# Linear attention and gated layers on one core: the last token pair's queries computed as seven block products, and output sums in place of query projections as filling ahead of the output weights

## The chip, the cores and the metric

The kernel runs on one core of a Trainium2 chip. The metric is device microseconds of one execution; lower is better. I name the engines as the profile does: PE is TensorE's matmuls, PEld its weight loads, DVE is VectorE, ACT is ScalarE, POOL is GpSimd, SP is SyncE, which issues the transfers. "L1237" is a line of the kernel that was profiled, so the same code has another number in another kernel.

## The reference, cut to what matters

Two layers are applied twice: a linear-attention layer A, then a gated layer B, on 2048 tokens of width 1024, 32 heads of 32.

```
def _A_ref(x, wqkv, wo):
    qkv = split_heads(x @ wqkv); q, k, v = qkv
    pq, pk = phi(q), phi(k)          # phi(t) = (t+1 if t>0 else exp(t)) + 1e-6
    kv  = einsum("bhsd,bhse->bhde", pk, v)
    z   = einsum("bhsd->bhd", pk)
    num = einsum("bhqd,bhde->bhqe", pq, kv)
    den = einsum("bhqd,bhd->bhq", pq, z)[..., None] + 1e-6
    return merge_heads(num / den) @ wo
x = x + A(layernorm(x)); x = x + B(layernorm(x))      # and both again
```

## The kernel before

In an attention layer, the queries and keys of a pair of token tiles (128 tokens each) are computed as a "quad": a 2 by 2 block product with seven instead of eight block products of 4 matmuls each, so 28 matmuls instead of 32. All pairs of the second layer and the last four of the first go this way, except the **queries of the last pair**, which are held back as four direct projections of 8 matmuls.

Then the keys are folded with the tokens ("G sums", 16 chunks), G with the value weights ("kv products"), and kv, masked to the heads by VectorE, with the output weights wo to give the combined output weights wp. Last come the output sums: 16 token tiles with two halves of 8 matmuls each. The end of that stage is where the held projections serve as filling:

```
            ph = proj("q", *held[0])          # 8 matmuls
            kvt(2 * KT - 1)                   # last kv product, then VectorE masks it
            ph()
            proj("q", *held[1])()             # 8 matmuls
            for g in range(4, 8):             # 4 output weights, 1 matmul each
                wprod(g, [0, 4, 1, 3][g - 4], g % 2 == 0)
            proj("q", *held[2])()
            for g in range(4, 8):
                wprod(NG + g, [0, 2, 1, 3][g - 4], g % 2 == 0)
            proj("q", *held[3])()
            # ...
            def y_grp(i, dh, n):              # output sum: 8 matmuls into one PSUM bank
                # dh 0: VectorE adds x and evicts; dh 1: ScalarE has seeded the bank with x and evicts
```

While the output sums run, the next layernorm runs beside them (statistics on VectorE, 1/sqrt on GpSimd, normalising on ScalarE), each normalised tile is transposed by a transfer, and VectorE builds block sums of the transposed tiles for layer B.

Of the kernel before, what the change touches and what calls it, by code (L numbers as in the profile page):

```python
# [180 lines left out]
def build_kernel(nc, A_x, A_wqkv, A_wo, B_w_gate, B_w_up, B_w_down, out):  # L181
    _, S, D = A_x.shape
    F = B_w_gate.shape[1]
    NST, NSB, KT, NG, NFT, NDH = S // 128, S // 512, D // 128, D // 128, F // 128, D // 512
# [8 lines left out]
    NHOLD = 2  # L193
# [52 lines left out]
    O_WP = RA  # L246
# [39 lines left out]
    P = _Prog(V_TW + 8 * 32)  # L286
# [39 lines left out]
    with ExitStack() as es:  # L326
# [19 lines left out]
        x_res = vb(O_X, NST * D).rearrange("p (i d) -> p i d", d=D)  # L346
        xnT = vh(O_XT, KT * S).rearrange("p (k s) -> p k s", s=S)
# [35 lines left out]
        def psb(b):  # L383
            return ps[:, b, :]
# [5 lines left out]
        B_TP = 3  # L390
        B_G = [0, 4]
        B_KVT = [1, 2]
        B_Z = [5, 6]
        B_YY = [5, 6, 7, 3]
        B_GX = [0, 1]
        B_GY = [2, 3]
# [15 lines left out]
        def r_x(i, lo=0, hi=D):  # L412
            return [(O_X + (i * D + lo) * 2, O_X + (i * D + hi) * 2)]
# [7 lines left out]
        def r_xT(s0, s1):  # L421
            return _seg(O_XT, KT, S * 2, s0 * 2, s1 * 2)

        def r_w(base, lo, hi):
            return _seg(base, KT, D * 2, lo * 2, hi * 2)
# [4 lines left out]
        def mset(ap, v, rng):  # L430
# [5 lines left out]
              rd=R(O_A[0], 1024), pwr=[B_KVT[1]])  # L436
# [473 lines left out]
        def layer_A(lnp, nxt, first):  # L910
            kq_i = [0]
            tok = lnp.order
# [19 lines left out]
            def proj(kind, i, h, mid=None):  # L932
                t, v, c0, base = WSRC[kind]
                bank = B_KQ[kq_i[0] % len(B_KQ)]
                kq_i[0] += 1

                def ev():
                    phi_evac(bank, *dst_of(kind, i, h))
                    if kind == "k" and tok.index(i) % 2 and h:
                        z_pair(tok.index(i) // 2)  # L940

                def part(ks):
                    P.add("pe", lambda e: [e.matmul(psb(bank), xnT[:, k, i * 128:(i + 1) * 128], t[:, k, h * 512:(h + 1) * 512],
                                                    start=(k == 0), stop=(k == KT - 1)) for k in ks],
                          rd=r_xT(i * 128, (i + 1) * 128)[ks[0]:ks[-1] + 1] + r_w(base, h * 512, (h + 1) * 512)[ks[0]:ks[-1] + 1], pwr=[bank])
                if mid == "parts":
                    return part, ev
                for ks in ((range(0, 4), range(4, 8)) if mid else (range(KT),)):
                    P.add("pe", (lambda ks: lambda e: [e.matmul(psb(bank), xnT[:, k, i * 128:(i + 1) * 128], t[:, k, h * 512:(h + 1) * 512],  # L949
                                                                start=(k == 0), stop=(k == KT - 1)) for k in ks])(ks),  # L950
                          rd=r_xT(i * 128, (i + 1) * 128) + r_w(base, h * 512, (h + 1) * 512)[ks[0]:ks[-1] + 1], pwr=[bank])
                    if mid:
                        mid()
                        mid = None
                return ev

            class Quad:
                n = 0

                def __init__(self, kind, p):  # L960
                    n = Quad.n
                    Quad.n += 1
                    self.kind, self.p = kind, p
                    self.X, self.Z, self.Y = QX[n % 2], QZ[n % 2], QY[(n + NPL) % 3]
                    self.u2 = (u2sb[n % 2], R(O_U2[n % 2], 2048))
                    self.u3 = (u3sb, R(O_U3, 2048))
                    self.i, self.i2 = tok[2 * p], tok[2 * p + 1]
# [208 lines left out]
            for p in range(npr, 6):  # L1176
                items += [("k", p), ("q", p)]
            if npr < 8:
                items += [("k", 6), ("k", 7), ("q", 6)]
            jobs = {}  # L1180

            def job(n, j, f):
# [43 lines left out]
                g_part(0, j)  # L1226

            QL = [Quad(kind, p) for kind, p in items]
            held = [(tok[i], h) for i in range(NST - NHOLD, NST) for h in range(2)]

            def g_part(n, j):
                h, jj = n // KT, n % KT
# [26 lines left out]
            def kvt(n):  # L1259
                h, j = n // KT, n % KT  # L1260

                def fn(e):
                    return [e.matmul(psb(B_KVT[h])[:, g * 128:(g + 1) * 128], wvs[j][:, (4 * h + g) * 128:(4 * h + g + 1) * 128],  # L1263
                                     GT[n % 4][:, g * 128:(g + 1) * 128],
                                     start=(j == 0 and g == 0), stop=(j == KT - 1), skip_group_check=True) for g in range(4)]
                P.add("pe", fn, rd=R(O_GT + n % 4 * 1024, 1024) + R(O_WVS[j] + h * 1024, 1024), pwr=[B_KVT[h]])
                if j == KT - 1:
                    P.add("dve", lambda e: e.tensor_tensor(
                        out=kvT[:, 4 * h:4 * h + 4, :], in0=psb(B_KVT[h]).rearrange("p (g c) -> p g c", c=128),
                        in1=mask.unsqueeze(1).broadcast_to([128, 4, 128]), op=ALU.mult),  # L1270
                        prd=[B_KVT[h]], rd=R(O_MASK, 256), wr=R(O_KVT + h * 1024, 1024))
# [16 lines left out]
            def wprod(n, bank, on_act):  # L1288
# [7 lines left out]
                else:  # L1296
                    P.add("dve", lambda e: e.tensor_scalar(out=dst, in0=psb(bank), scalar1=rz[:, g:g + 1], scalar2=None, op0=ALU.mult),
                          prd=[bank], rd=R(O_RZ, 32), wr=wr)

            for n in range(2 * KT):  # L1300
                if n:
                    gchunk(n)
                if first and n % 2 == 0:
                    pack()
                if n == 2:
                    z_final()
                if n == 4:
                    z_col()
                if n >= 1:
                    kvt(n - 1)  # L1310
                if n >= KT + 2:
                    m = n - KT - 2
                    for d in range(2):
                        if m < 4:
                            wprod(d * NG + m, B_Z[d], True)
                if n >= 2 and na[0] < NNORM:
                    norm(tok[na[0]])
                    na[0] += 1
            ph = proj("q", *held[0])
            kvt(2 * KT - 1)  # L1320
            ph()
            proj("q", *held[1])()
            for g in range(4, 8):
                wprod(g, [0, 4, 1, 3][g - 4], g % 2 == 0)
            proj("q", *held[2])()
            for g in range(4, 8):
                wprod(NG + g, [0, 2, 1, 3][g - 4], g % 2 == 0)
            proj("q", *held[3])()

            def y_seed(n):  # L1330
                if n < NST:
                    xs, bank = x_res[:, tok[n], 512:1024], B_YY[(2 * n + 1) % 4]
                    P.add("act", lambda e: e.copy(psb(bank), xs), rd=r_x(tok[n], 512, 1024), pwr=[bank])

            def y_grp(i, dh, n):
                bank = B_YY[(2 * n + dh) % 4]

                def fn(e):
                    return [e.matmul(psb(bank), xnT[:, g, i * 128:(i + 1) * 128], wp[:, g, dh * 512:(dh + 1) * 512],  # L1339
                                     start=(dh == 0 and g == 0), stop=(g == NG - 1), skip_group_check=True) for g in range(NG)]  # L1340
                xs = x_res[:, i, dh * 512:(dh + 1) * 512]
                rx = r_x(i, dh * 512, (dh + 1) * 512)
                P.add("pe", fn, rd=r_xT(i * 128, (i + 1) * 128) + r_w(O_WP, dh * 512, (dh + 1) * 512), pwr=[bank])
                if dh == 0:
                    P.add("dve", lambda e: e.tensor_tensor(out=xs, in0=psb(bank), in1=xs, op=ALU.add), prd=[bank], rd=rx, wr=rx)
                    return
                P.add("act", lambda e: e.copy(xs, psb(bank)), prd=[bank], wr=rx)

            nxt.use_dma = True
            nxt.on_act = YACT  # L1350
            ring_begin(first)
            for _ in range(3):
                ring_issue()
            y_seed(0)
            for i in range(NST):
                if na[0] < NST:
                    if i % 3 == 2:
                        norm(tok[na[0]])
                        na[0] += 1
                elif RG["n"] < NR:  # L1360
                    ring_issue()
                if first and i % 3 == 1:
                    pack()
                nxt.step_t(1)
                nxt.b1_one()
                if 2 <= i < 15:
                    nxt.start(i - 2)
                y_grp(tok[i], 0, i)
                y_seed(i + 1)
                if i < 15:  # L1370
                    nxt.b2_one()
                y_grp(tok[i], 1, i)
                if first and i >= 14:
                    prep_s(i - 14)
                if not first and i >= 8:
                    stash(i - 8)
                if nxt.t_next >= 8 and RG["tq"] is None:
                    RG["tq"] = t_ops(0)
                for _ in range(2 if i > 12 else 1):
                    if RG["tq"]:  # L1380
                        RG["tq"].pop(0)()
# [691 lines left out]
```

## Time and profile before

| | before |
|---|---|
| time, median of 3 runs | 1428.89 us (1428.35 to 1429.38) |
| profiled run | 1428.16 us, span 1426.4 us |
| matmul records / weight loads | 8150 / 8209 |
| first quad to first matmul of layer B, first attention layer | 168.03 us |
| the same, second attention layer | 217.37 us |

Every matmul has one weight load, so 59 matmul records of this trace are lost. That is why I measure stages from the start of one matmul to the start of another and do not count matmul records: the second layer's first quad matmul is one of the lost ones, and it is set one slot (0.216 us) before the first recorded. The prediction shows the lines of the page and of TensorE's timeline that matter; the profiled run of before, at 1428.16 us, was, as it will turn out, faster than every other run of this kernel on record (the next is 1428.35).

### The profile page before, as it was taken

The page shows a single profiled execution, that of the slowest core. Times are in us where ns is not written, and L with a number is a line of the kernel's source. Part 1 is how long each engine was busy: PE and PEld are TensorE (multiplying, and loading weights), DVE is VectorE, ACT ScalarE, POOL GpSimd, SP SyncE. Part 2 cuts the span into 40 slices and gives each one's busy share as a digit, 9 for nine tenths or more (in the row PEclk, how much of TensorE's full clock was granted, in tenths as well). Part 3 has the DMA queues.
Part 4 walks back from the last instruction along what each step waited for, and adds up shares of the span by engine and source line. Part 5 has one row for each costly group of instructions (what it writes and reads, how often), then busy time and mean ns, then how long its engine had stood idle before and what let it go on. Part 6 is the DMA issues. An engine that isn't in the chain of part 4 may idle for free.

```text
span 1426.4 us, 21923 instructions
## 1 busy us (share of the span) xinstructions
PE 1417.6 (99%) x8150; PEld 791.0 (55%) x8209; DVE 1200.9 (84%) x2344; ACT 722.0 (51%) x1471; POOL 153.8 (11%) x197
## 2 busy tenths in 40 slices
PE   9999999999999999999999999999999999999999
PEld 4444444555546566664554444456666475666548
DVE  7897978999978799987689978788888877888888
ACT  5882355444420266655377814567776105777400
POOL 3203521000010000002010045310000100000000
PEclk9999999999999999999999999999999999999999
DMA  7868978997786777768884367767775966777553
GB/s 240 218 141 225 216 179 197 310 311 265 252 264 212 234 254 249 252 228 295 239 281 104 92 177 162 172 196 254 258 246 194 329 221 230 259 258 260 191 205 122
DMA packets 270699, 320.74 MB, mean 225 GB/s; under 512 B 164096, under 2 KB 211072, under 8 KB 270592
## 3 DMA queue, kind: packets, MB, share of 16 engines
q1 hardware_dynamic: 270592, 319.34, 73.2%
q8 instruction: 64, 1.05, 0.3%
q14 instruction: 43, 0.35, 0.1%
HBM read 236.45 MB, written 73.40 MB: 217 GB/s over the span
## 4 chain that ended last, share of the span: by engine, by line
PE 92%; DVE 4%; ACT 2%; issue 1%; DMA 1%; POOL 0%; SPq 0%; DVEq 0%
PE ps L1421 29%; PE ps L1504 17%; PE ps L1853 16%; PE ps L1339 8%; PE ps L1237 8%; PE ps L976 8%; PE ps L1760 5%; DVE arena L808 1%; PE ps L949 1%; DVE arena L811 1%; DVE arena L455 1%; ACT arena L668 1%; DMA arena<-in_A_wqkv_dram 1%; PE ps L1263 1%; PE ps L1290 0%
## 5 line engine op out<-in xcount | busy, mean ns | idle before, releaser
L808 DVE TENSOR_TENSOR arena<-arena 128x512 f16<-128x512 f16 (+7 forms) x1027 | 507.3, 522 | 56.9 <-ACT arena L1508 32.7
L1421 PE MATMUL ps<-arena 128*128 128x512 f16 x1888 | 456.8, 379 | 0.1
L811 DVE SCALAR_TENSOR_TENSOR arena<-ps,arena 128x512 f16<-128x512 f32 (+3 forms) x558 | 358.6, 658 | 86.9 <-PE ps L1853 45.0
L1504 PE MATMUL ps<-arena 128*128 128x256 f16 x2184 | 287.5, 273 | 0.1
L1421 PEld LDWEIGHTS ps<-arena 128*128 128x128 f16 (+1 forms) x1888 | 182.9, 98 | 162.4 <-ACT ps L1450 3.8
L1504 PEld LDWEIGHTS ps<-arena 128*128 128x128 f16 (+1 forms) x2184 | 212.3, 98 | 90.4 <-ACT arena L1508 7.2
L1853 PE MATMUL ps<-arena 128*128 128x512 bf16 (+1 forms) x1048 | 230.6, 379 | 0.8
L1853 PEld LDWEIGHTS ps<-arena 128*128 128x128 f16 x1064 | 104.1, 98 | 123.8
L1426 ACT ACTIVATE arena<-ps 128x512 f32<-128x512 f32 x224 | 133.9, 598 | 76.7 <-PE ps L1421 62.5
L1508 ACT ACTIVATE arena<-ps 128x256 f32<-128x256 f32 x351 | 125.1, 384 | 26.4 <-PE ps L1504 21.5
L976 PE MATMUL ps<-arena 128*128 128x512 f16 (+1 forms) x605 | 134.0, 379 | 1.2 <-ACT arena L983 0.6
L1237 PE MATMUL ps<-arena 128*128 128x512 bf16 x498 | 114.7, 379 | 0.7
L1339 PE MATMUL ps<-arena 128*128 128x512 bf16 x502 | 110.3, 379 | 0.5
L1514 ACT COPY ps<-ps 128x256 f32<-128x256 f32 x182 | 66.3, 364 | 75.5 <-DVE arena L811 28.5
L976 PEld LDWEIGHTS ps<-arena 128*128 128x128 f16 x616 | 59.3, 98 | 74.8 <-ACT arena L983 5.9
L1760 PE MATMUL ps<-arena 128*128 128x256 f16 (+1 forms) x882 | 97.0, 273 | 0.0
L1450 ACT COPY ps<-ps 128x512 f32<-128x512 f32 x112 | 65.4, 583 | 61.5 <-PE ps L1421 51.3
L1078 POOL TENSOR_TENSOR arena<-arena 128x1024 f16<-128x1024 f32 x32 | 77.2, 2413 | 155.7 <-DVE arena L1076 140.8
L1760 PEld LDWEIGHTS ps<-arena 128*128 128x128 f16 x882 | 86.2, 98 | 11.0 <-DVE arena L811 0.2
L1517 DVE TENSOR_TENSOR ps<-ps,arena 128x256 f32<-128x256 f32 x182 | 76.7, 428 | 10.7 <-PE ps L1504 9.5
L1339 PEld LDWEIGHTS ps<-arena 128*128 128x128 f16 x512 | 50.1, 98 | 60.4
L1788 ACT COPY arena<-ps 128x256 f32<-128x256 f32 x8 | 3.0, 373 | 155.8 <-PE ps L1760 155.8
(72 smaller groups left out, 981.0 us busy)
## 6 DMA issues: line engine op xcount, KB each, us to landing
arena<-w_scratch SPq DMA_DIRECT2D x84, 896.0 KB, 4.6
arena<-t_scratch SPq DMA_DIRECT2D x32, 896.0 KB, 5.9
arena<-in_B_w_down_dram SPq DMA_DIRECT2D x24, 896.0 KB, 5.0
arena<-sp_scratch SPq DMA_DIRECT2D x26, 768.0 KB, 4.2
w_scratch<-arena SPq DMA_DIRECT2D x28, 512.0 KB, 6.1
arena<-w_scratch SPq DMA_DIRECT2D x28, 384.0 KB, 4.7
x_scratch<-arena SPq DMA_DIRECT2D x40, 256.0 KB, 5.1
arena<-x_scratch SPq DMA_DIRECT2D x40, 256.0 KB, 4.1
```

What stands on the lines that cost most here:

```text
L808: P.add("dve", lambda e: e.tensor_tensor(out=out, in0=a, in1=b, op=op), rd=rd, wr=wr, prd=prd)
L811: P.add("dve", lambda e: e.scalar_tensor_tensor(out=out, in0=a, scalar=sc, in1=b, op0=ALU.mult, op1=op1), rd=rd, wr=wr, prd=prd)
L976: P.add("pe", lambda e: [e.matmul(psb(bank), a[0][:, k, :], b[0][:, k, :], start=(q in (1, 5) and k == 0), stop=(k == 3), skip_group_check ...
L1078: P.add("pool", lambda e: e.tensor_tensor(out=asb[b].rearrange("p (h c) -> p h c", c=32), in0=pbuf.rearrange("p (h c) -> p h c", c=32), in ...
L1237: return [e.matmul(psb(bank), xrt[t][:, jj * 128:(jj + 1) * 128], pk[:, h, t, :], start=(t == tok[0]), stop=(t == tok[NST - 1])) for t in ts]
L1339: return [e.matmul(psb(bank), xnT[:, g, i * 128:(i + 1) * 128], wp[:, g, dh * 512:(dh + 1) * 512], start=(dh == 0 and g == 0), stop=(g == ...
L1421: P.add("pe", lambda e: [e.matmul(psb(bank), w[:, k, :], x[:, k, :], start=(start and k == 0), stop=(k == 3), skip_group_check=True) for k ...
L1426: P.add("act", lambda e: e.activation(t, psb(bank), AF.Copy, scale=SG), prd=[bank], wr=r)
L1504: P.add("pe", lambda e: [e.matmul(psb(bank)[:, 256 * half:256 * half + 256], w[:, k, :], xx[:, k, :], start=(start and k == 0), stop=(k == ...
L1508: P.add("act", lambda e: e.activation(d, src, AF.Copy, scale=sc), prd=[xk], wr=rd_)
L1760: P.add("pe", lambda e: [e.matmul(psb(bank)[:, 256 * half:256 * half + 256], a[:, k, 128 * r:128 * r + 128], b[:, k, :], start=(start and ...
L1853: P.add("pe", lambda e: [e.matmul(psb(bank), hv[:, 7 * hf + k, t * 128:(t + 1) * 128], w[:, k, :], start=(q in "15" and hf == 0 and k == 0 ...
```

## The change

The intent: the last pair's queries become a quad as well (28 matmuls in place of 32), and the wait for the output weights is filled with the first halves (4 of 8 matmuls) of the output sums of tiles 0 and 1. Those can start early, because the first four output weights of each half are ready long before. Two more PSUM banks stay open meanwhile, so banks are dealt anew.

```diff
-        B_Z = [5, 6]
+        B_Z = [5, 3]
...
-                    self.X, self.Z, self.Y = QX[n % 2], QZ[n % 2], QY[(n + NPL) % 3]
+                    self.X, self.Z, self.Y = QX[n % 2], QZ[n % 2], QY[(n + NPL + 2) % 3]
...
-                items += [("k", 6), ("k", 7), ("q", 6)]
+                items += [("k", 6), ("k", 7), ("q", 6), ("q", 7)]
...
             for n in range(2 * KT):
+                if n == 2 * KT - 1:
+                    y_seed(0)
+                    y_seed(1)
...
-            ph = proj("q", *held[0])
-            kvt(2 * KT - 1)
-            ph()
-            proj("q", *held[1])()
-            (output weights, held[2], output weights, held[3] as shown above)
+            def y_part(n, dh, k):
+                y_mm(n, dh, range(4 * k, 4 * k + 4))
...
+            y_part(0, 0, 0)
+            y_part(0, 1, 0)
+            kvt(2 * KT - 1)
+            y_part(1, 0, 0)
+            for g in range(4, 8):
+                wprod(g, [0, 1, 4, 2][g - 4], g % 2 == 0)
+            y_part(1, 1, 0)
+            for g in range(4, 8):
+                wprod(NG + g, [0, 1, 4, 2][g - 4], g % 2 == 0)
```

(In the loop of output sums, tiles 0 and 1 then run their second halves only; that part is cut.)

More of the change, by code (lines that the diff above doesn't have):

```diff
@@ L1228, in layer_A @@
             QL = [Quad(kind, p) for kind, p in items]
-            held = [(tok[i], h) for i in range(NST - NHOLD, NST) for h in range(2)]
             def g_part(n, j):
@@ L1298, in wprod, with y_seed @@
                           prd=[bank], rd=R(O_RZ, 32), wr=wr)
+            def y_seed(n):
+                if n < NST:
+                    xs, bank = x_res[:, tok[n], 512:1024], B_YY[(2 * n + 1) % 4]
+                    P.add("act", lambda e: e.copy(psb(bank), xs), rd=r_x(tok[n], 512, 1024), pwr=[bank])
             for n in range(2 * KT):
+                if n == 2 * KT - 1:
+                    y_seed(0)
+                    y_seed(1)
                 if n:
@@ L1318, in layer_A, with y_mm @@
                     na[0] += 1
-            ph = proj("q", *held[0])
-            kvt(2 * KT - 1)
-            ph()
-            proj("q", *held[1])()
-            for g in range(4, 8):
-                wprod(g, [0, 4, 1, 3][g - 4], g % 2 == 0)
-            proj("q", *held[2])()
-            for g in range(4, 8):
-                wprod(NG + g, [0, 2, 1, 3][g - 4], g % 2 == 0)
-            proj("q", *held[3])()
-            def y_seed(n):
-                if n < NST:
-                    xs, bank = x_res[:, tok[n], 512:1024], B_YY[(2 * n + 1) % 4]
-                    P.add("act", lambda e: e.copy(psb(bank), xs), rd=r_x(tok[n], 512, 1024), pwr=[bank])
+            def y_mm(n, dh, gs):
+                i, bank = tok[n], B_YY[(2 * n + dh) % 4]
+                P.add("pe", lambda e: [e.matmul(psb(bank), xnT[:, g, i * 128:(i + 1) * 128], wp[:, g, dh * 512:(dh + 1) * 512],
+                                                start=(dh == 0 and g == 0), stop=(g == NG - 1), skip_group_check=True) for g in gs],
+                      rd=r_xT(i * 128, (i + 1) * 128)[gs[0]:gs[-1] + 1] + r_w(O_WP, dh * 512, (dh + 1) * 512)[gs[0]:gs[-1] + 1], pwr=[bank])
+            def y_part(n, dh, k):
+                y_mm(n, dh, range(4 * k, 4 * k + 4))
             def y_grp(i, dh, n):
                 bank = B_YY[(2 * n + dh) % 4]
-                def fn(e):
-                    return [e.matmul(psb(bank), xnT[:, g, i * 128:(i + 1) * 128], wp[:, g, dh * 512:(dh + 1) * 512],
-                                     start=(dh == 0 and g == 0), stop=(g == NG - 1), skip_group_check=True) for g in range(NG)]
+                if n < 2:
+                    y_part(n, dh, 1)
+                else:
+                    y_mm(n, dh, range(NG))
                 xs = x_res[:, i, dh * 512:(dh + 1) * 512]
                 rx = r_x(i, dh * 512, (dh + 1) * 512)
-                P.add("pe", fn, rd=r_xT(i * 128, (i + 1) * 128) + r_w(O_WP, dh * 512, (dh + 1) * 512), pwr=[bank])
                 if dh == 0:
@@ L1353, in layer_A @@
                 ring_issue()
-            y_seed(0)
             for i in range(NST):
@@ L1367, in layer_A @@
                     nxt.start(i - 2)
-                y_grp(tok[i], 0, i)
-                y_seed(i + 1)
+                if i != 1:
+                    y_grp(tok[i], 0, i)
+                if i == 0:
+                    y_grp(tok[1], 0, 1)
+                else:
+                    y_seed(i + 1)
                 if i < 15:
```

## The prediction

> **What bounds the kernel now.** I read the page first, for the busy shares and the chain that ended last, then the list of what TensorE waited for, then the two stretches that the change rewrites, in order of time.
>
> ```profile
> span 1426.4 us, 21923 instructions
> PE 1417.6 (99%) x8150; PEld 791.0 (55%) x8209; DVE 1200.9 (84%) x2344; ACT 722.0 (51%) x1471; POOL 153.8 (11%) x197
> PE 92%; DVE 4%; ACT 2%; issue 1%; DMA 1%; POOL 0%; SPq 0%; DVEq 0%
> ...
> PE ps L435 <- POOL arena L431: 1.4, 1, 1.4
> PE ps L943 <- DMA arena<-in_A_wqkv_dram: 0.7, 2, 0.5
> PE ps L976 <- ACT arena L983: 0.6, 3, 0.2
> ```
>
> TensorE (PE) is busy 99% of the span and carries 92% of the chain. Over the whole span its waits come to 2.7 us, of which 2.1 us are at the start of the kernel. So there is almost no idle time left to win: a change is worth the matmuls that it takes off TensorE, less any new wait.
>
> The stretch in question, first linear-attention layer, from the timeline of TensorE (start, length, engine, line, instructions; the lengths include the drain of the last matmul, so I use differences of starts):
>
> ```profile
> 165.77 3.62 PE L1237 MATMUL ps<-arena 128*128 128x512 bf16 x16
> 169.22 0.39 PE L1263 MATMUL ps<-arena 128*128 128x128 bf16 x4
> 169.44 1.89 PE L949 MATMUL ps<-arena 128*128 128x512 bf16 x8
> 171.17 0.39 PE L1263 MATMUL ps<-arena 128*128 128x128 bf16 x4
> 171.39 1.89 PE L949 MATMUL ps<-arena 128*128 128x512 bf16 x8
> 173.12 1.03 PE L1290 MATMUL ps<-arena 128*128 128x512 bf16 x4
> 174.20 1.67 PE L949 MATMUL ps<-arena 128*128 128x512 bf16 x7
> 175.71 1.03 PE L1290 MATMUL ps<-arena 128*128 128x512 bf16 x4
> 176.57 1.89 PE L949 MATMUL ps<-arena 128*128 128x512 bf16 x8
> ```
>
> L1237 is the last G sum, L1263 the kv products, L949 the four query projections of the last token pair that were held back as filling, L1290 the output weights; the output sums L1339 begin at 178.30. Eight L949 matmuls take 171.17 - 169.44 = 1.73 us, so one slot is 0.216 us; four short ones take 0.22 us. The stretch from 169.22 to 178.30 holds 32 + 8 matmuls of 512 columns (one record is missing, the "x7") and 8 of 128: 40 x 0.2157 + 8 x 0.056 = 9.08 us, and it lasts 9.08 us. The second layer shows the same 9.07 us (878.55 to 887.62). So the wait for the output weights **is already filled without a gap**; the change cannot win there, it can only fill it with other work.
>
> **What the Trainium skill says.** "TensorE: Matmul & The Clock Gate", section "Back-to-back issue gap", gives N/2.4 + 2.5 ns, 216 ns for 512 columns; the trace agrees (0.216 us). The 131 ns that the same section gives for a sustained stream does not appear here. The same page, "Step-by-step: what each phase is for", says that weight loads are pulled ahead of running matmuls; here they start 0.21 us ahead (172.91 against 173.12). "Perfetto Trace Analysis", section "Tensor Engine Instruction (MATMUL, LD_WEIGHTS)", says that matmul ends are estimated, hence my use of starts. "PSUM — Partial Sum Buffer", section "The four PSUM rules", says that writes of ScalarE leave the accumulate bits alone: the second half of an output tile is seeded by a ScalarE copy of x and then summed without a clearing first matmul, and two more banks now stay open across the weight products. This matters for correctness, not time; no run so far shows it.
>
> **The change, part by part (per attention layer; there are two).**
>
> 1. Removed: four direct projections, 4 x 8 = 32 matmuls, 32 x 0.2157 = 6.90 us.
> 2. Added: one more quad (seven block products of 4 matmuls, 28 in all), 28 x 0.2157 = 6.04 us. It needs no new operand sums: the key quad of the same pair makes them already and now keeps them one step longer. Net of 1 and 2: **-4 matmuls, -0.86 us**.
> 3. Moved: 16 of the 256 output-sum matmuls, 3.45 us, from behind the output weights to before and between them. No net change on TensorE.
> 4. The new wait. Before, 1.73 us of queries lie between the last kv product and the first output weight. That weight needs the masked kv matrix. The rows of the timeline between:
>
> ```profile
> 171.59 0.69 DVE L1268 TENSOR_TENSOR arena<-ps,arena 128x512 bf16<-128x512 f32 x1 [1.38 <-PE ps L1263]
> ...
> 176.34 0.10 PEld L1290 LDWEIGHTS ps<-arena 128*128 128x128 bf16 x1 [0.31 <-DVE arena L1297]
> ```
>
> VectorE (DVE) ends the mask at 171.59 + 0.69 = 172.28. A weight load released by VectorE starts 0.05 us after it (L1297 ends at 176.29, the load starts at 176.34) and its matmul hardly later (176.36). So the output weight could have run at about 172.34, which is 1.17 us after the kv products began at 171.17. In the new order there are 0.22 us of kv products and only four output-sum matmuls (0.86 us), 1.09 us in all. **New stall: about 0.09 us.** VectorE is free for it in time: it idled 1.38 us before this row, and the 0.22 us kv group before it sits at the same distance from the last G sum as now.
> 5. The second group of weights reuses banks 0, 1, 4, 2 of the first. Let t be the start of the first. Matmuls end at t+0.38, +0.60, +0.81, +1.03; two VectorE evictions take 1.40 us as a pair (row L1297, "1.40 ... x2" in the timeline), so the last bank is free near t + 0.64 + 1.40 = t + 2.04. It is needed at t + 0.86 + 0.86 + 0.65 = t + 2.37. No stall, 0.3 us to spare, and ScalarE with 1.26 us a pair is earlier. Before, both engines evicted queries in this window as well; that load is gone. The second half of tile 0's second output half needs the weights of the second group: ready near t + 2.32 + 0.04 + 1.40 = t + 3.76, needed at t + 4 x 0.86 + 0.86 = t + 4.3. No stall.
> 6. The extra quad's evictions come in the quad stage, where TensorE has this beside it (columns: stretch, its length, then busy us and count of PE, PEld, DVE, ACT, POOL):
>
> ```profile
> 725.00:815.64 90.64, 89.63 (x410) 40.03 (x417) 80.51 (x200) 72.31 (x132) 4.58 (x10) 1.00 0.48 135
> 169.22:178.30 9.08, 9.03 (x48) 4.29 (x48) 6.57 (x13) 4.69 (x8) 2.48 (x2) 1.00 1.11 200
> ```
>
> Fifteen quads: VectorE 80.51/15 = 5.4 us and ScalarE 72.31/15 = 4.8 us per quad, against 6.04 us of TensorE. Both fit. The 412 matmuls from 725.55 to 815.48 should take 88.87 us and take 89.93: three stalls of some 0.35 us behind ScalarE's copy L983, in quads that also carry layernorm work. The new quad is the last and has none, so I put 0.03 us on it.
> 7. Banks: turning the Y banks by two puts the first quad of the second layer on bank 2. In the preceding layer's last evictions this bank is read by the one that starts at 724.87 and ends at 725.55; the quad needs it at 726.0. No stall.
>
> Sum: 2 x (-0.86 + 0.09 + 0.03) = -1.5 us. **1428.9 - 1.5 = 1427.4 us**, 0.1% faster.
>
> **The rivals.**
> A. A new wait takes the place of the old filling. Filling between kv and the weights is halved, from 1.73 to 0.86 us, and VectorE works in order: one late normalisation (3.3 us of VectorE work per tile) ahead of the mask would show at once. For it: DVE is 84% busy. Against it: it idled 1.4 us (first layer) and 2.1 us (second layer) before the mask. If it holds, up to 0.9 us a layer are lost and the time stays at 1428.9.
> B. The evictions become the bound. The projections needed 4 plain evictions; a quad also needs three PSUM copies on ScalarE. If the last quad lasts 6.9 us in place of 6.04, nothing is gained: 1428.9 to 1429.5. Against it: the loads in step 6.
> C. Relief downstream: fewer evictions in the weights' window, so that the output sums start cleaner. TensorE shows no gap there before, so there is nothing to relieve: same as my number. Even if every wait at L976 (about 1 us with the drain) vanished as well, 1426.3 would be the floor.
> D. Transfers. The reload of a block of query weights, needed by the projections alone, is left in. 512 KB a layer were hidden before and stay hidden; no effect on the time.
>
> **Range and chances.** My centre is the count of matmuls, which is firm, less small stalls, which are not. C bounds it below near 1426.4; A or B in full brings it back to 1428.9. The three runs before span 1.0 us, so I add some on top: 1426.4 to 1428.9. A change of 2% is 28.6 us; the work touched is some 20 us a layer, so faster by 2% is all but excluded, and slower by 2% needs a stall that I have overlooked: 0.003 and 0.007.
>
> **What would show it.** Right: the matmuls of line L949 fall by 64 and those of L976 rise by 56; the stretch from last G sum to the rest of the output sums shrinks from 9.08 to about 5.7 us, with one gap of about 0.1 us ahead of the first output weight, released by the mask on VectorE; the quad stage grows by about 6.0 us; the output sums after the weights shrink by 3.45 us. Wrong: a gap of 0.3 us or more before the output weights or between their groups, new waits of L976 on ScalarE in the last quad, or a first G sum that waits for a bank.

## The result

| | before | after |
|---|---|---|
| median | 1429.14 us (1428.35 to 1429.71, 4 runs) | 1426.71 us (1426.61 to 1427.38, 4 runs) |
| ratio | | 0.9984, 95% interval 0.9967 to 1.0002 |
| first attention layer, first quad to layer B | 168.03 us | 167.26 us |
| second attention layer, same | 217.37 us | 216.57 us |

A ratio is the mean time of one kernel's fast runs over that of the other's of the same rounds, so it is not quite the ratio of the medians.

From the page of after, the head and the busy line:

```profile
span 1425.7 us, 21979 instructions
PE 1419.6 (100%) x8201; PEld 790.6 (55%) x8201; DVE 1201.3 (84%) x2348; ACT 726.9 (51%) x1481; POOL 154.2 (11%) x197
```

There are 8 matmuls fewer (8201 weight loads against 8209), yet PE's busy time rose by 2 us. Nothing got slower: this trace lost no matmul record and the earlier one lost 59. Here the span and the stages say more than the busy sum.

TensorE's timeline of after in the stretch that the prediction shows (start, length, engine, line, count; L1262 is kv, L1328 output sums, L1289 output weights), and then the weight load and the mask at the first output weight, with the idle time before them in brackets:

```profile
175.77 0.39 PE L1262 MATMUL ps<-arena 128*128 128x128 bf16 x4
175.99 1.89 PE L1328 MATMUL ps<-arena 128*128 128x512 bf16 x8
177.72 0.39 PE L1262 MATMUL ps<-arena 128*128 128x128 bf16 x4
177.94 1.03 PE L1328 MATMUL ps<-arena 128*128 128x512 bf16 x4
178.89 1.04 PE L1289 MATMUL ps<-arena 128*128 128x512 bf16 x4
179.76 1.03 PE L1328 MATMUL ps<-arena 128*128 128x512 bf16 x4
...
178.14 0.69 DVE L1267 TENSOR_TENSOR arena<-ps,arena 128x512 bf16<-128x512 f32 x1 [0.35 <-PE ps L1262]
178.89 0.55 PEld L1289 LDWEIGHTS ps<-arena 128*128 128x128 bf16 x4 [0.41 <-DVE arena L1267]
```

Four output-sum matmuls begin at 177.94 and should be issued by 177.94 + 4 x 0.2157 = 178.80; the first output weight starts at 178.89. That is the one gap, 0.085 us in the unrounded starts, released by the mask. Between the two groups of weights there is none (178.89 + 4 x 0.2157 = 179.76). The second layer has the same single gap.

**Where the time went.** The two attention layers are 0.77 and 0.80 us shorter, 1.57 us in all. But the profiled pair differs by only 0.8 us (1428.16 against 1427.38) and the medians by 2.4 us. Three things outside these stages move between runs: the stretch before the first quad (65.2 to 66.1 us over all profiles; 0.51 us longer in this profile of after), the last stage (0.27 us shorter in after), and a gap of 0.55 us at the **hand-over** from the first attention layer to layer B. With the two layers they add up to the 0.8 us of the profiled pair. The timelines of TensorE there, first before, then after (L1421 and L1434 are the same line, layer B's first matmuls):

```profile
237.65 6.65 PE L1421 MATMUL ps<-arena 128*128 128x512 f16 x30
```

```profile
237.82 3.40 PE L1434 MATMUL ps<-arena 128*128 128x512 f16 x15
241.61 2.76 PE L1434 MATMUL ps<-arena 128*128 128x512 f16 x12 [0.39 <-DVE arena L811]
```

Before ran through; after waits for VectorE. From start to start the gap is 0.767 us where one slot is 0.216: 0.55 us lost. What VectorE was doing, from its timeline of after, with its first eviction for layer B (L811) as the last row:

```profile
217.95 0.69 DVE L1345 TENSOR_TENSOR arena<-ps,arena 128x512 bf16<-128x512 f32 x1 [1.07 <-PE ps L1328]
221.33 1.23 DVE L808 TENSOR_TENSOR arena<-arena 128x2048 f16<-128x2048 f16 x1 [2.69 <-DMA arena<-arena]
...
240.87 0.68 DVE L811 SCALAR_TENSOR_TENSOR arena<-ps,arena 128x512 f16<-128x512 f32 x1
```

VectorE sat idle for 2.69 us until a transfer landed, the transpose of the eighth normalised tile, and then worked without a gap until 240.87. In before the same two times are 221.03 and 240.58. So the saving of the first attention layer can be swallowed here. That became the question of the experiments.

### The profile page after: what moved, and what is told of

Its sections match the earlier page's. It is cut to its first block, busy times and chain, and to the rows that moved or that the text cites. A ratio compares the mean times of both kernels' runs of the same rounds, so it can differ in the third digit from the quotient of the medians.

```text
span 1425.7 us, 21979 instructions
## 1 busy us (share of the span) xinstructions
PE 1419.6 (100%) x8201; PEld 790.6 (55%) x8201; DVE 1201.3 (84%) x2348; ACT 726.9 (51%) x1481; POOL 154.2 (11%) x197
## 4 chain that ended last, share of the span: by engine, by line
PE 95%; DVE 3%; DMA 1%; issue 1%; ACT 0%; SPq 0%; DVEq 0%
PE ps L1434 28%; PE ps L1517 17%; PE ps L1866 16%; PE ps L976 9%; PE ps L1236 8%; PE ps L1773 7%; PE ps L1328 6%; PE ps L949 3%; DVE arena L808 1%; DMA arena<-in_A_wqkv_dram 1%; PE ps L1262 1%; PE ps L1289 0%; DVE arena L455 0%; DVE arena L996 0%; PE ps L943 0%
## 5 line engine op out<-in xcount | busy, mean ns | idle before, releaser
L808 DVE TENSOR_TENSOR arena<-arena 128x512 f16<-128x512 f16 (+9 forms) x1035 | 510.4, 521 | 58.0 <-ACT arena L1521 32.8
L1434 PE MATMUL ps<-arena 128*128 128x512 f16 x1888 | 457.0, 379 | 0.5 <-DVE arena L811 0.4
L811 DVE SCALAR_TENSOR_TENSOR arena<-ps,arena 128x512 f16<-128x512 f32 (+3 forms) x558 | 358.1, 657 | 87.3 <-PE ps L1866 44.3
L1434 PEld LDWEIGHTS ps<-arena 128*128 128x128 f16 (+1 forms) x1888 | 183.0, 98 | 162.8 <-ACT ps L1463 3.8
L1866 PEld LDWEIGHTS ps<-arena 128*128 128x128 f16 x1064 | 104.1, 98 | 123.8
L976 PE MATMUL ps<-arena 128*128 128x512 f16 (+1 forms) x672 | 146.8, 379 | 0.6 <-ACT arena L983 0.6
L1236 PE MATMUL ps<-arena 128*128 128x512 bf16 x512 | 116.1, 379 | 0.0
L1328 PE MATMUL ps<-arena 128*128 128x512 bf16 x512 | 111.8, 379 | 0.0
L976 PEld LDWEIGHTS ps<-arena 128*128 128x128 f16 x672 | 64.8, 98 | 81.4 <-ACT arena L983 6.1
L1773 PEld LDWEIGHTS ps<-arena 128*128 128x128 f16 x882 | 86.2, 98 | 11.0 <-DVE arena L811 0.2
L1328 PEld LDWEIGHTS ps<-arena 128*128 128x128 f16 x512 | 49.9, 98 | 59.5
```

The lines of the kernel that those rows point to most:

```text
L808: P.add("dve", lambda e: e.tensor_tensor(out=out, in0=a, in1=b, op=op), rd=rd, wr=wr, prd=prd)
L811: P.add("dve", lambda e: e.scalar_tensor_tensor(out=out, in0=a, scalar=sc, in1=b, op0=ALU.mult, op1=op1), rd=rd, wr=wr, prd=prd)
L976: P.add("pe", lambda e: [e.matmul(psb(bank), a[0][:, k, :], b[0][:, k, :], start=(q in (1, 5) and k == 0), stop=(k == 3), skip_group_check ...
L1236: return [e.matmul(psb(bank), xrt[t][:, jj * 128:(jj + 1) * 128], pk[:, h, t, :], start=(t == tok[0]), stop=(t == tok[NST - 1])) for t in ts]
L1328: P.add("pe", lambda e: [e.matmul(psb(bank), xnT[:, g, i * 128:(i + 1) * 128], wp[:, g, dh * 512:(dh + 1) * 512], start=(dh == 0 and g == ...
L1434: P.add("pe", lambda e: [e.matmul(psb(bank), w[:, k, :], x[:, k, :], start=(start and k == 0), stop=(k == 3), skip_group_check=True) for k ...
```

## The experiments

All variants come from one source with switches. With the switches set as in before and as in after, its instruction sequence on each of the five engines is that of before and of after. Every kernel ran 5 rounds. All outputs are right. "Before" is the kernel before in the same call, on the same chip.

| kernel | median, us | mean | before, mean | ratio | 95% interval |
|---|---|---|---|---|---|
| *first call* | | | | | |
| after_again | 1426.94 | 1427.12 | 1429.18 | 0.9985 | 0.9973 to 0.9998 |
| first_only | 1428.14 | 1428.10 | 1429.18 | 0.9992 | 0.9979 to 1.0005 |
| second_only | 1428.15 | 1427.90 | 1429.18 | 0.9991 | 0.9978 to 1.0003 |
| quad_no_fill | 1432.55 | 1432.87 | 1429.18 | 1.0022 | 1.0008 to 1.0035 |
| *second call* | | | | | |
| before_again | 1429.11 | 1429.24 | 1429.03 | 1.0002 | 0.9988 to 1.0015 |
| no_reload | 1428.03 | 1428.19 | 1429.03 | 0.9994 | 0.9982 to 1.0007 |
| late_noreload | 1427.59 | 1427.81 | 1429.03 | 0.9991 | 0.9979 to 1.0004 |
| relu_split | 1430.50 | 1430.37 | 1429.03 | 1.0009 | 0.9997 to 1.0022 |
| *third call* | | | | | |
| after_third | 1427.73 | 1427.70 | 1429.19 | 0.9989 | 0.9977 to 1.0002 |
| no_reload_2 | 1428.00 | 1428.04 | 1429.19 | 0.9992 | 0.9979 to 1.0004 |
| act_adds | 1427.29 | 1427.34 | 1429.19 | 0.9986 | 0.9972 to 0.9999 |
| before_act_adds | 1429.36 | 1429.37 | 1429.19 | 1.0001 | 0.9988 to 1.0014 |

The means are of all five runs; the ratios agree with their quotient to 0.0001, except for quad_no_fill, where the ratio fits the mean without the slowest run, 1432.33. The intervals are about as wide as the effects, so most conclusions below rest on stages of the profiles, which repeat to 0.03 us where nothing disturbs them. There is one profile for each row, so a row cannot tell its kernel from its run.

From each profile I worked out, from starts of matmuls: **A0** and **A1**, the first and second attention layer from the first quad to layer B's first matmul; **landing**, when VectorE starts its first block sum, counted from the first quad; **gap**, what TensorE loses in the first 9 us of layer B.

| kernel | first layer | A0 | landing | gap | A1 |
|---|---|---|---|---|---|
| before | old | 168.03 | 155.51 | 0 | 217.37 |
| before_again | old | 168.03 | 156.49 | 0.98 | 217.37 |
| second_only | old | 168.03 | 156.15 | 0.64 | 216.60 |
| first_only | new | 167.26 | 155.32 | 0.58 | 217.37 |
| after | new | 167.26 | 155.30 | 0.55 | 216.57 |
| after_again | new | 167.26 | 155.14 | 0.41 | 216.59 |
| after_third | new | 167.26 | 156.05 | 1.29 | 216.59 |
| no_reload | new | 167.44 | 156.24 | 1.32 | 216.59 |
| no_reload_2 | new | 167.28 | 156.01 | 1.24 | 216.59 |
| late_noreload | new | 167.16 | 155.84 | 1.20 | 216.51 |
| relu_split | new | 167.16 | 156.38 | 1.73 | 218.90 |

(The profiles of the third call miss the record of the second layer's first quad matmul; A1 is corrected by one slot there, as for before.)

### The changed kernel again, and each layer alone

after_again is the changed kernel. The other two use the old path in one of the two layers:

```diff
 def layer_A(lnp, nxt, first):
+    new = first          # first_only;  new = not first for second_only
     ...
-    items += [("k", 6), ("k", 7), ("q", 6), ("q", 7)]
+    items += [("k", 6), ("k", 7), ("q", 6)] + ([("q", 7)] if new else [])
     # likewise the banks, the filling and the loop of output sums
```

> The changed kernel again, for a firmer number. Theory 1, count: four matmuls fewer and a 0.085 us stall more per attention layer, all of it kept, 1.5 us faster than before. Theory 2, hand-back: the profile of after shows a new gap of 0.55 us (starts 240.84 to 241.61 in place of one slot) at the hand-over from the first attention layer to the gated layer, where TensorE waits for VectorE, so only about 1.0 us is kept. Theory 3: the 2.4 us between the medians of the first runs are real and something is won that I did not see. Whether the gap near 241 us comes again tells if it belongs to the kernel or to that run.

> The change in the first attention layer alone. Theory 1: 0.77 us faster. Theory 2: the gap at the hand-over (near 241 us) is there, 0.2 to 0.4 us faster. Theory 3: some 1.2 us.

> The change in the second attention layer alone. Theories 1 and 2: 0.6 to 0.8 us faster, no gap at the hand-over in the first layer. Theory 3: some 1.2 us.

Measured by means: 2.06, 1.08 and 1.28 us faster than the kernel before. The parts add up to 2.36, which is 2.06 within the noise, so **each layer carries about half**. The stages of the profiles follow theory 1 exactly: A0 is 167.26 wherever the first layer is new and 168.03 where it is old, A1 216.6 and 217.37. But the gap of theory 2 is also there, and it is there in second_only, whose first layer is the old one. So the change does not cause it: my theory 2, in that form, fell. The gain in the means is larger than 0.77 us a layer, as theory 3 has it, but by less than the half width of the intervals (some 1.8 us), and these three runs do not say why.

### The quad without the filling

```diff
-            y_part(0, 0, 0)
-            y_part(0, 1, 0)
             kvt(2 * KT - 1)
-            y_part(1, 0, 0)
             for g in range(4, 8):
                 wprod(g, [0, 1, 4, 2][g - 4], g % 2 == 0)
-            y_part(1, 1, 0)
             for g in range(4, 8):
                 wprod(NG + g, [0, 1, 4, 2][g - 4], g % 2 == 0)
     # the seeding with x and the loop of output sums are as in before again (cut)
```

> The seven block products for the last pair in both layers, but no output sums ahead of the weights: nothing fills the waits. Worked out from durations in the trace, per layer: the last kv product waits 0.62 us for ScalarE's copy of the G sum, the first output weight 0.95 us for the mask, the second group of weights 0.58 us in all for banks; with 0.86 us fewer matmuls this makes 1.3 us a layer slower, 2.6 us in all. The rival, that the filling matters little because VectorE or the transfers set the end of the stage anyway, expects the same time as before or faster.

It is 3.7 us slower than before by the means of all five runs (3.2 without its slowest, the profiled one at 1435.04 us), and over 5 us slower than the changed kernel. The rival is refuted: the filling carries the change. In the second layer my sum holds: A1 grows from 217.37 to 218.69 us, 1.32 us for an expected 1.3. In the first layer of the profiled run A0 grows by 3.77 us. The timeline there shows the rest (L1281 kv, L1308 output weights, L1286 the mask, L1092 a step of the normalisation on VectorE, L1096 its multiplication on GpSimd):

```profile
176.11 1.91 POOL L1096 TENSOR_TENSOR arena<-arena 128x1024 f16<-128x1024 f32 x1 [2.68 <-DMA arena<-arena]
176.22 1.83 DVE L1092 TENSOR_SCALAR arena<-arena 128x32 f32<-128x32 f32 x1
176.71 0.23 PEld L1281 LDWEIGHTS ps<-arena 128*128 128x128 bf16 x4 [0.62 <-ACT arena L1261]
...
178.36 0.63 DVE L1286 TENSOR_TENSOR arena<-ps,arena 128x512 bf16<-128x512 f32 x1
179.04 0.55 PEld L1308 LDWEIGHTS ps<-arena 128*128 128x128 bf16 x4 [2.11 <-DVE arena L1286]
```

The wait for ScalarE's copy is 0.62 us as reckoned. The wait for the mask is 2.1 us, not 0.95, because a small VectorE step, 0.46 us on average in after, took 1.83 us beside GpSimd's multiplication and stood in front of the mask. (At this place it took 1.54 us in after as well; there it was over before the mask's input was ready.) The Trainium skill, "SBUF — State Buffer", section "Who interferes with whom", describes a port pair that VectorE and GpSimd share as a lock, "the other **fully blocks** (not throttle)"; the row agrees, it ends 0.04 us after GpSimd's; no run here tests it by moving one of the two. The waits seem to have had a second price, from the view by stretches (stretch, its length, busy us of PE, PEld, DVE, ACT, POOL, then granted clock, DMA share, GB/s; the number of instructions in brackets):

```profile
176.00:179.70 3.70, 1.30 (x12) 0.61 (x10) 2.93 (x5) 0.81 (x2) 3.09 (x2) 1.00 1.26 216
179.70:183.20 3.50, 3.37 (x10) 1.04 (x9) 2.91 (x4) 3.21 (x6) 0.74 (x1) 0.55 1.15 284
```

The two waits, close together, were followed by 3.5 us at a clock of 0.55, in which matmuls started every 0.427 us in place of 0.216. That the waits caused it is not shown. It is not so in every run: such a drop takes 0.45 x 3.5 / 1433 = 0.001 off the mean clock of the span, and only the profiled run and one other, the two slowest, have 0.999; the other three have 1.000. So rival A of the prediction is real: with no filling at all it comes true. In the changed kernel the mask had 0.35 us of idle VectorE ahead of it in the first layer; that is how close it is.

### The kernel before as a control

No edit; the kernel before from the common source.

> The kernel before, instruction for instruction, as a control. Its first profile ran 1428.16 us, the fastest of all its runs, and shows no gap at the hand-over from the first attention layer to the gated layer (near 241 us), where four profiles of other kernels show 0.41 to 0.64 us. Theory 2 (the change causes that gap): no gap here either, span of the stages as in the first profile. Theory 2b (the gap belongs to that hand-over and to the run, whatever the kernel; the first profile was a lucky one): a gap of 0.4 us or more here, and the stage between the two attention layers near 492.4 us in place of 492.0. Ratio 1.000 within 0.0006.

The ratio is 1.0002, and the gap is there:

```profile
237.65 3.83 PE L1488 MATMUL ps<-arena 128*128 128x512 f16 x17
242.30 1.90 PE L1488 MATMUL ps<-arena 128*128 128x512 f16 x8 [0.82 <-DVE arena L827]
```

TensorE loses 0.98 us there. Theory 2b holds: **the profile on which the prediction rests was a lucky run**, and the "never waits" that I read from it is not true of the kernel in general.

### The reload of the query weights left out, twice

```diff
-            dma(wq[:, 0:4, 512:1024], wqkv_v[:, 0:4, 512:1024], ..., KW["q"][1])
```

> The changed kernel without the reload of the block of query weights (512 KB a layer), which nothing reads any more. If the gap at the hand-over is a matter of transfer traffic, it shrinks from 0.4 to 0.6 us to under 0.2 us and the time falls by 0.4 us against the changed kernel, to a ratio near 0.9982. If the traffic has nothing to do with it: same gap, ratio 0.9985.

> The changed kernel without the reload, again, now beside the changed kernel on the same chip. In its first run the gap grew to 1.12 us and the ratio was 0.9994, but on another chip than the changed kernel's. If the chip made that, it equals the changed kernel here within 0.0003; if leaving the reload out does it (the transfers behind it move and meet others), the tile lands 0.6 us or more later than in the changed kernel again, gap near 1.1 us, ratio near 0.9992.

The first run went against the expectation: the gap did not shrink, it was 1.32 us. (The 1.12 us in the expectation of the repeat is the second of the two gaps that make it up.) The repeat stood beside the changed kernel on one chip, and there the two are alike: landing 156.01 and 156.05, gap 1.24 and 1.29 us, ratios 0.9992 and 0.9989. So the first run's gap belongs to the chip, the call or the run, which these runs cannot tell apart, and leaving the reload out changed nothing beside the changed kernel, as the prediction's rival D says.

The first run shows something else. Its A0 is 0.18 us longer than in after, because the stall before the first output weight is 0.26 us there in place of 0.085; in no_reload_2 it is 0.10. The small VectorE step of the section on quad_no_fill took 1.78 and 1.54 us in these two, and the mask followed it and the reciprocal without any idle time. So the 0.35 us ahead of the mask can be used up in the changed kernel too: the instructions of all engines but SyncE are the same in no_reload and in after.

### A longer filling before the first output weight

On top of no_reload:

```diff
             y_part(0, 0, 0)
-            y_part(0, 1, 0)
             kvt(2 * KT - 1)
+            y_part(0, 1, 0)
             y_part(1, 0, 0)
```

> As no_reload, and one of the two partial output sums that stand ahead of the last kv product goes behind it, so that the filling before the first output weight is 1.73 us again and before the kv product 1.09 us. My arithmetic of the stall: both gaps of 0.085 us before the output weights vanish, each attention layer is 0.085 us shorter (167.26 and 216.58 us become 167.17 and 216.50). The kv product needs ScalarE's copy of the G sum about 0.85 us after the last G matmul was issued, so 1.09 us is enough. The rival, that the gap comes from something else than the length of the filling, keeps it.

Both gaps are gone (L1281 kv, L1356 output sums, L1308 output weights):

```profile
176.84 0.39 PE L1281 MATMUL ps<-arena 128*128 128x128 bf16 x4
177.07 1.89 PE L1356 MATMUL ps<-arena 128*128 128x512 bf16 x8
178.79 1.03 PE L1308 MATMUL ps<-arena 128*128 128x512 bf16 x4
```

177.07 + 8 x 0.2157 = 178.79 within rounding, with nothing lost. A0 and A1 are 0.10 and 0.06 us shorter than in after, where 0.085 was reckoned; the kv product between the halves did not wait either. The time cannot show 0.2 us.

### Relief for ScalarE in the second layer's quads

On top of late_noreload:

```diff
-    RLB = [(4, 5, 6, 7), (4, 5, 6, 7)]     # banks whose positive part ScalarE takes
+    RLB = [(4, 5, 6, 7), (4, 7)]
```

> As late_noreload, and in the second layer the positive part of one of the two banks of each quad is taken by VectorE straight from PSUM and not by ScalarE's extra pass. If the three gaps of some 0.35 us in the second layer's quads come from ScalarE's queue (4.8 of 6.04 us a quad, plus the layernorm's), they vanish and the second attention layer shrinks by 1.0 us, ratio near 0.9975. The rival: VectorE (5.4 us a quad, some 5.8 then) becomes what TensorE waits for, and nothing is won or time is lost.

The rival was right. The three gaps behind ScalarE are gone, but TensorE waits for VectorE (L693 is VectorE's eviction straight from PSUM), from the list of TensorE's waits (total, times, longest):

```profile
PE ps L994 <- DVE arena L693: 2.8, 3, 1.2
```

A1 is 218.90 us, 2.4 us longer than late_noreload's. Averaged over the quad stage VectorE's work grew by only 0.2 us, from 5.4 us a quad (79.97 us beside 414 matmuls, 28 a quad) to 5.6 (81.02 beside 404) of 6.04, so it is not the average that reaches the limit; the waits come at three single places.

### Relief for VectorE at the hand-over, in both kernels

```diff
+    ADDS = (12, 13)                    # first layer only
     # tiles in ADDS: the bank of half 0 is seeded with x by ScalarE, as half 1 always is,
     # the first matmul doesn't clear it, and ScalarE evicts it
-                if dh == 0:
+                if dh == 0 and n not in ADDS:
                     (VectorE adds x and evicts)
```

act_adds is the changed kernel with this and the longer filling; before_act_adds is the kernel before with this alone. after_third is the changed kernel for comparison.

> The changed kernel once more, on the chip of the next three runs. Known so far: at the hand-over from the first attention layer to the gated layer VectorE's first eviction ends a chain that is packed for 19.57 us from the landing of one transposed tile, in every profile; TensorE waits there if the tile lands late. Theory 2c: counted from the first quad, the tile lands near 155.2 us in the changed kernel (155.1 to 155.3 in three profiles) and near 156.0 in the kernel before (155.5 to 156.5), so that the first layer's gain arrives in full or more in most runs; gap 0.3 to 0.6 us, ratio 0.9984. If it lands near 156 us here, the difference between the chips, not the change, makes it, and the ratio is nearer 0.9990.

> The changed kernel with the later filling of late_noreload (reload kept), and in the first layer the first output half of tiles 12 and 13 is seeded and evicted by ScalarE, so that two additions of 0.65 us leave VectorE's packed chain: 19.57 becomes about 18.3 us, the gap at the hand-over vanishes, and the two stalls before the output weights too. Expected 0.5 to 0.7 us under the changed kernel, ratio near 0.9980. If ScalarE's four extra passes of 0.58 us hold back the layernorm instead, the tile lands later and nothing is won.

> The kernel before with only that relief of VectorE. If typical runs of the kernel before lose 0.5 to 1.0 us at the hand-over, which its first profile did not show, this takes it away: ratio near 0.9994, no gap near 241 us. If the first profile was typical, same time as before, ratio 1.000.

after_third has landing 156.05 and gaps of 1.29 us: theory 2c fell, the changed kernel's landing is not always near 155.2. Both reliefs failed: gaps of 1.22 us (act_adds) and 0.75 us (before_act_adds) remain. VectorE's timeline of act_adds says why:

```profile
226.46 0.21 DVE L503 TENSOR_SCALAR arena<-arena 128x1 f32<-128x1 f32 x1 [0.76 <-POOL arena L482]
226.59 1.41 DVE L471 BATCH_NORM_STATS2 arena<-arena 128x6 f32<-128x512 bf16 x2
...
230.93 0.21 DVE L503 TENSOR_SCALAR arena<-arena 128x1 f32<-128x1 f32 x1 [0.46 <-POOL arena L482]
```

The two additions are gone, 1.3 us, and 0.76 + 0.46 = 1.22 us of idle time stands in their place: VectorE now waits for GpSimd's steps of the layernorm. Those are normally short (0.22 and 0.57 us); beside VectorE's large block sum they took 1.08 and 1.40 us:

```profile
228.34 1.08 POOL L476 TENSOR_SCALAR arena<-arena 128x1 f32<-128x1 f32 x1 [1.91 <-DVE arena L475]
229.50 1.40 POOL L482 TENSOR_TENSOR arena<-arena 128x1 f32<-128x1 f32 x1
```

So the chain at the hand-over is not VectorE's work alone; the layernorm's path through GpSimd, held up beside VectorE's own block sums, has nearly the same length. Taking one away leaves the other.

### Which version is best

By means act_adds is 0.36 us faster than the changed kernel on the same chip (1427.34 against 1427.70) and its A1 (216.50 after the same correction) is as short as late_noreload's. The two intervals overlap almost wholly, so I don't claim it as better.

## Why the prediction was right, and where it was only half right

The prediction was 1427.4 us, 1.5 us faster. The first runs gave 1426.71, the repeats 1426.94 and 1427.73: all within its range. By means the change gains 2.23, 2.06 and 1.49 us in the three sets.

**Removed and added matmuls.** Right. Weight loads of L949 fell from 288 to 224 and of L976 rose from 616 to 672, a net of -8 in two layers.

**The stretch.** Right: the stretch between the last G sum and the output sums shrank from 9.08 to 5.72 us in the first layer, the quad stage grew from 40.80 to 46.84 us and the output sums after the weights shrank from 55.25 to 51.80 us.

**The new stall.** Right in both layers of after: 0.09 us reckoned, 0.085 measured, and late_noreload took it away by lengthening the filling, which shows its cause. The margin behind it was thinner than I reckoned: I counted 1.38 us of idle VectorE ahead of the mask as in before, and found 0.35 in after, 1.69 in after_third and none in no_reload, where the stall was 0.26 us.

**The second group of weights.** Right: no gap, though without filling (quad_no_fill) there are some.

**The extra quad.** Right: the three gaps of 0.35 us in the second layer's quads are there again and no fourth came.

**The banks.** Right: no wait at the first quad of either layer.

**The sum.** -0.86 + 0.09 + 0.03 makes -0.74 per layer, against A0 -0.77 and A1 -0.80 us; the 0.03 for the last quad did not come. The attention layers are what I reckoned.

**The step that failed** is the dismissal in rival C: "TensorE shows no gap there before, so there is nothing to relieve", and with it the premise that the matmul count of the first layer arrives in the time. In the table above, every row obeys one rule within 0.03 us: A0 + gap = landing + 12.52. (before: 168.03 + 0 = 155.51 + 12.52; after_third: 167.26 + 1.29 = 156.05 + 12.50.) VectorE is packed for 19.54 to 19.55 us from the landing to the start of its first eviction, so where there is a gap, layer B goes on at a time that **the landing of the eighth transposed tile sets, not TensorE**. The first layer's 0.77 us are then worth just as much as the landing comes earlier. The lucky profile of before lay exactly at the edge, gap 0. That the total still came within my range is therefore partly luck: the landing moved in the right direction, and nothing in the prediction says that it would.

Within a call, kernels with a new first layer have an earlier landing than the one with the old one, by 0.8 to 1.0 us in the first call (155.14 and 155.32 against 156.15) and by 0.25 and 0.65 in the second (156.24 and 155.84 against 156.49). The third call has no profile of an unedited old first layer to compare with.

The landing moves by up to 0.9 us between calls for the same kernel (155.14 and 156.05), and the traces show where. In every profile of the table SyncE issues the transpose of the eighth tile 0.05 us after its issue of the seventh ends, and by then the eighth tile has been normalised for 0.4 to 1.9 us. So it waits for SyncE, which is still issuing the seventh, and not for the layernorm. The transposes' line in the stretch from 212 to 219 us, after_again and then after_third (number of issues, then the shortest, the median and the longest in ns):

```profile
L579 SPq DMA_TRANSPOSE arena<-arena x5: 1231/1307/2017, 210.9 to 218.9; - x5
L579 SPq DMA_TRANSPOSE arena<-arena x4: 1307/1316/2957, 211.5 to 218.6; - x4
```

The longest in each is the seventh tile's, 2.02 and 2.96 us where the others there take 1.2 to 1.3: 0.94 us more, which covers the difference. Counted from the first quad this issue begins at 149.25 to 149.87 us in the rows with a new first layer and at 149.76 to 150.41 us in those with the old one, so the change tends to bring it forward; but it lasts 1.9 to 3.4 us in the one and 2.1 to 2.9 us in the other. What makes it long I did not find; leaving out 512 KB of transfers did not do it. **That stays open**, and with it the part of the 2 us that goes beyond 1.57. The stretch before the first quad and a single gap of 0.25 us in the last stage, which comes and goes (it is in before and before_again, and not in after), vary as well; no run ties them to the change.

**The rivals.** A (a new wait in place of the filling) came as 0.085 us a layer, and as 0.26 us in one layer of no_reload; quad_no_fill shows what it costs in full. B (evictions as the bound) did not come; relu_split shows that some 0.2 us more VectorE work a quad brings waits of 2.8 us in all in the second layer. D (transfers hidden) held.

## What to carry to other kernels

Where an engine is busy 99% of the time, count its instructions: the count and one overlap worked out from durations gave the two stages to 0.03 us. But take more than one profile of the kernel before as the base, for a run that lies on the edge of a wait looks as if the wait did not exist. And before one counts on a saving, follow the next hand-over back to what sets it; relieving one engine there only uncovered a second chain of the same length.

## What the Trainium skill lacked or had wrong

- "TensorE: Matmul & The Clock Gate", section "Back-to-back issue gap": the 131 ns for a sustained stream of 512-column matmuls never appears; in after 240 output-sum matmuls in a row run at 0.216 us each, which is the formula that the page gives for an isolated one, and no matmul starts less than 0.215 us after one of 512 columns.
- The same page, section "Why this matters for your kernels", advises against idle gaps over some 3 us. In quad_no_fill two waits of 0.62 and 2.1 us, 0.2 us of matmuls apart, were followed by 3.5 us at a clock of 0.55 in the profiled run; the second layer's waits of 0.62 and 0.95 us were not (the page speaks of short idles elsewhere, but gives no length for them).
- "SBUF — State Buffer", section "Who interferes with whom", describes the lock but not what it does to tiny instructions on a critical chain: GpSimd's one-column steps went from 0.22 and 0.57 to 1.08 and 1.40 us, a VectorE step on 32 columns from 0.46 (mean) to 1.83 us. That the lock is the cause is read from the overlap of the rows alone.
- None of the pages drawn on here gives the time from VectorE's end to the weight load that it releases; the trace shows 0.05 us, and the matmul follows within 0.02 us.
